# A fused FFT, MLP and routed-expert kernel: GpSimd's small operations one a step, and a shorter routing chain on VectorE

## The chip, the cores and the metric

One Trainium2 chip, one of its NeuronCores. The metric is the device time of one execution in microseconds (us). Three runs of the kernel before gave 3348.24, 3348.84 and 3351.0 us; the median is 3348.84 us. The engines are called PE (TensorE), DVE (VectorE), ACT (ScalarE), POOL (GpSimd) and SP (SyncE, which issues most transfers).

## What is computed

```python
X = np.fft.fft(x, axis=1); X = np.fft.fft(X, axis=2)     # x: 8 x 3072 x 256
x = X.real.reshape(24576, 256)
h = x @ w_in                                             # 256 -> 2048
g = h * np.clip(h + 3, 0, 6) / 6
x = g @ w_out                                            # 2048 -> 256
logits = x @ w_gate                                      # 8 experts
expert_idx = np.argmax(logits, axis=1)
probs = np.exp(logits - logits.max(-1, keepdims=True))
probs /= probs.sum(-1, keepdims=True) + 1e-09
# each token goes to its one expert: relu(x @ w1[e]) @ w2[e], times its probability
```

## The kernel before

The program has two parts. The first, to about 2150 us, does the Fourier transforms, the MLP and the routing; it ends with every token's row stored in a DRAM table `xs_dram` that is sorted by expert. The second reads tiles of that table and applies the experts. The change touches the first part alone.

**Batches, chunks, steps.** The first part runs over 8 batches, each of 6 chunks of 512 tokens, each of 8 steps: 384 steps in all. A step `s` (`step`, from L942) does for one pair of the 16 slices of the hidden width:

- PE: `mm1` writes the step's two halves into the PSUM tile `ab` (14 products with `WA`, `WB`, `XN`), and `mm2` of three steps before (LAG = 3) multiplies `gh` and `gl` with `WO` into `acc` (24 products, L513). `ab` has two buffers, which the transforms' products (`f`, `fe`, `fo`) and the routing's products share.
- ACT copies one half to `A` (L496); DVE makes `h` with a difference (L184) and a sum (L181) of `A` and `ab`; ACT makes `r` (L501), DVE multiplies it by `h` (L508), ACT rounds the product to `gh` (L959), and POOL writes what was rounded off to `gl` (L184, two operations a step). `r` has four buffers, two a step, so ACT's `r` of a step needs the buffer that `gl` of two steps before reads.

**Fill work.** Lists by step (`fill`, `pfill`, `afill`) hold everything else. For the next batch's transform `plan_folds` (L697) puts 40 operations of DVE on chosen steps: the folds of four input quarters `R` (774 or 516 columns), of their sums `H`, and splits into `SC0`, `SC1`, `SS0`, `SS1`. After a quarter's four folds POOL makes four sums `H<-R`, all in the step after the last fold. `R` has two buffers; SP loads a quarter when the sums of the quarter two before have been made.

**Routing** (`routing`, L542) follows each chunk: `s0` (maximum, difference, exponential), `s1` (one-hot `rt_oh` of the chosen expert), `s2` (POOL: running counts `rt_oc`, `cnt`), four steps later `s3_mm` (PE: rank of each token within its expert, two products) and `s3` (DVE: base + rank, times the one-hot, summed over experts to a row number `pi`; the sum of the exponentials and its reciprocal; the destination copied into the row), and four times `s4` (POOL: an indirect store of 128 rows of `xp` to `xs_dram`).

**Order.** A scheduler sets each engine's order from the program and its own estimate of readiness, except for what is pinned (`in_order`, `keep_in_program_order`: the folds stay in the written order among themselves). Each engine then works strictly in its order.

Of the kernel before, what the change touches and what calls it, by code (L numbers as in the profile page):

```python
# [10 lines left out]
F32 = mybir.dt.float32  # L11
# [35 lines left out]
BUFS = dict(h=2, r=4, gh=4, gl=4)  # L47
EXTRA = 23
LATE = (0, 0, 1, 1, 2, 3, 3, 4, 5, 5, 6, 6, 7, 7, 8, 8, 8, 9)
# [25 lines left out]
def tile_fft_moe(ctx, tc, xr, xf, xcoef, w_in, w_out, w_gate, w1, w2, tabs, fm, misc, tri, sgn8, dstc, maskc, out):  # L75
# [55 lines left out]
    w128 = pc.tile([P, KF], F32, name="w128")  # L131
    trib = pc.tile([P, P], BF16, name="trib")

# [4 lines left out]
    ssel = pc.tile([P, 1], F32, name="ssel")  # L138
    base8 = pc.tile([P, 4, NE], F32, name="base8")
    iom8 = pc.tile([P, 4, NE], F32, name="iom8")  # L140
# [39 lines left out]
    def add(eng, o, a, b):  # L180
        pinned(eng.tensor_tensor(out=o, in0=a, in1=b, op=ALU.add))  # L181

# [161 lines left out]
    def load_consts():  # L344
        sp.dma_start(ident, misc[:, 0:P])
        sp.dma_start(iot, misc[:, P:P + 2])
        sp.dma_start(itile, misc[:, P + 2:P + 2 + NTILE])
        o = P + 2 + NTILE
        sp.dma_start(cmask, misc[:, o:o + 64].rearrange("p (a c) -> p a c", a=NE))
        o += 64  # L350
        sp.dma_start(base8, misc[:, o:o + 32].rearrange("p (a c) -> p a c", a=4))
        o += 32
        sp.dma_start(iom8, misc[:, o:o + 32].rearrange("p (a c) -> p a c", a=4))
        o += 32
        sp.dma_start(dst_sb, dstc)
# [186 lines left out]
    def routing(xo, xp, t0, nt, mask, tagn, wait=RKW):  # L542
# [5 lines left out]
        def s0():  # L548
            st["m"] = m = sm("rt_m", [P, 4])
            st["d"] = d = sm("rt_d", [P, 4, NE])  # L550
            dve.tensor_reduce(out=m[:, 0:nt], in_=L, axis=AX.X, op=ALU.max)
            dve.tensor_tensor(out=d[:, 0:nt], in0=L, in1=bc(m), op=ALU.subtract)
            st["ex"] = ex = sm("rt_ex", [P, 4, NE])
            act.activation(ex[:, 0:nt], d[:, 0:nt], AF.Exp)

# [11 lines left out]

        def s2():
            st["oc"] = oc = sm("rt_oc", [P, 4, NE], BF16)
            oh = st["oh"]  # L570
            pool.tensor_copy(oc[:, 0], cnt)
            for t in range(nt):
                o = oc[:, t + 1] if t + 1 < nt else cnt
                pool.tensor_tensor(out=o, in0=oc[:, t], in1=oh[:, t], op=ALU.add)

        def s3_mm():
            ab = hold["ride"][:, 1] if hold.get("ride") is not None else bank(f"rk{tagn}")
            st["r"] = r = ab[:, 384:384 + nt * NE]
            mm_group(r, [(trib, st["oh"][:, 0:nt].rearrange("p t e -> p (t e)")),
                         (onesb, st["oc"][:, 0:nt].rearrange("p t e -> p (t e)"))])  # L580

        def s3():
            k = st["k"]
            r = st["r"].rearrange("p (t e) -> p t e", e=NE)
            dve.tensor_tensor(out=k[:, 0:nt], in0=base8[:, 0:nt], in1=r, op=ALU.add)
            s = sm("rt_s", [P, 4])
            dve.tensor_reduce(out=s[:, 0:nt], in_=st["ex"][:, 0:nt], axis=AX.X, op=ALU.add)
            dve.tensor_tensor(out=k[:, 0:nt], in0=k[:, 0:nt], in1=st["oh"][:, 0:nt], op=ALU.mult)
            dve.tensor_scalar(s[:, 0:nt], s[:, 0:nt], 1e-9, None, op0=ALU.add)
            ps = sm("rt_p", [P, 4])  # L590
# [13 lines left out]

        return [("f", s0), ("f", s1), ("f", s2)] + [("f", lambda: None)] * wait + [("p", s3_mm, s3)] + [("f", lambda t=t: s4(t)) for t in range(nt)]

    if True:
# [94 lines left out]
        def plan_folds(b):  # L702
# [225 lines left out]
        def step(s):  # L928
# [21 lines left out]
            if 0 < s <= NS:  # L950
                h = hold.pop(("h", s - 1))
                r, gh, gl = halves("r", F32, s), halves("gh", F32R, s), halves("gl", F32R, s)
                g = r
                for n in range(2):
                    relu6(r[n], h[n])
                for n in range(2):
                    gate_h(g[n], r[n], h[n])
                for n in range(2):
                    act.activation(gh[n], g[n], AF.Copy)  # L959
                for n in range(2):  # L960
                    sub(pool, gl[n], g[n], gh[n])
                hold[("g", s - 1)] = (gh, gl)
# [179 lines left out]
def _constants():  # L1142
# [26 lines left out]
    for c in range(1, 128):  # L1169
# [7 lines left out]
            np.tile((np.arange(8)[None, :] <= np.arange(8)[:, None]).astype(float).reshape(1, 64), (P, 1)),  # L1177
            np.tile((np.arange(8.0) * CAPR + TS)[None, None], (P, 4, 1)).reshape(P, 32),
# [3 lines left out]
    tri = (p[:, None] < p[None, :]).astype(float)  # L1182
    sgn8 = np.where(p[None, :, None] // 2 == np.arange(NB)[:, None, None], (-1.0) ** n, 0.0)
# [96 lines left out]
```

## Time and profile before

| | |
|---|---|
| median of three runs | 3348.84 us |
| the profiled execution, its own time | 3351.21 us |
| its span, first to last instruction | 3349.4 us |
| busy in the span | PE 94%, DVE 68%, POOL 68%, ACT 58% |
| 350 to 1903 us, batches 1 to 6 | 1553 us: PE 1439.95 busy, DVE 1189.59, POOL 1112.91, ACT 991.01 |
| the same stretch, ACT waiting for POOL's `gl` | 151.0 us in 53 waits |

How to read it: busy time overlaps between engines, and a busy PE is not one at its peak, since matmuls are pipelined. The waits are put down to what came last. In the stretch from 350 to 1903 us the same pattern of 48 steps comes six times. In a timeline row the first number is the start, the second the duration, and the bracket the idle time of the engine before it with what ended it.

### The profile page before, as it was taken

The numbers are of one execution on the slowest core, as the hardware profiler recorded it, in microseconds if no ns is written. First come the engines' busy times: TensorE is split into PE (matmuls) and PEld (weight loads), VectorE is DVE, ScalarE is ACT, GpSimd is POOL, SyncE is SP. The second block draws the span as 40 slices with busy tenths as digits, with TensorE's granted clock in tenths as the row PEclk, the third lists the DMA queues.
The fourth block names the chain that finished last, engine by engine and source line by source line (L and its number), as shares of the span: only waits on it lengthen the run. The fifth ranks groups of instructions, "written<-read, shape, count | busy, mean of one in ns | idle before, by whom it ended". The sixth has DMA issues, their size and how long they took to land.

```text
span 3349.4 us, 62616 instructions
## 1 busy us (share of the span) xinstructions
PE 3133.1 (94%) x23482; PEld 3001.7 (90%) x23482; DVE 2277.1 (68%) x3699; ACT 1934.1 (58%) x3339; POOL 2267.7 (68%) x1784
## 2 busy tenths in 40 slices
PE   5899999999999999999899999999999999999998
PEld 5899999899899899899899999988888888898887
DVE  8878777777777777777777676755555555555553
ACT  3566666566666566666566666645454444544453
POOL 5567776776776777677777776766676666666664
PEclk8999999999999999999999999999999999999999
DMA  5100100100100110000000002065555555545560
GB/s 180 61 28 21 36 25 14 43 24 16 39 28 16 33 33 16 30 30 17 31 14 16 14 18 51 20 193 154 144 168 149 143 149 158 147 145 154 147 171 30
DMA packets 256195, 243.18 MB, mean 73 GB/s; under 512 B 157739, under 2 KB 219020, under 8 KB 255888
## 3 DMA queue, kind: packets, MB, share of 16 engines
q1 hardware_dynamic: 234640, 184.66, 19.7%
q0 software_dynamic: 21248, 54.48, 4.5%
q8 instruction: 187, 3.06, 0.4%
q14 instruction: 120, 0.98, 0.1%
HBM read 159.71 MB, written 54.04 MB: 64 GB/s over the span
## 4 chain that ended last, share of the span: by engine, by line
PE 45%; DVE 18%; ACT 17%; issue 9%; POOL 5%; SPq 0%; DMA 0%; ACTq 0%; POOLq 0%; DVEq 0%
PE op L165 16%; PE hp L165 15%; PE acc L513 8%; ACT gh L959 7%; ACT r L501 6%; PE ab L165 5%; DVE h L184 4%; POOL gl L184 3%; DVE r L508 2%; POOL xs_dram L149 2%; DVE R L189 2%; DVE R L181 2%; DVE H L181 1%; ACT xp L539 1%; ACT xo L532 1%
## 5 line engine op out<-in xcount | busy, mean ns | idle before, releaser
L184 POOL TENSOR_TENSOR gl<-r,gh 128x512 fp32r<-128x512 f32 x768 | 1109.6, 1464 | 468.1 <-ACT gh L959 372.7
L501 ACT ACTIVATE r<-h,half 128x512 f32<-128x512 f32 x768 | 546.4, 719 | 610.1 <-DVE h L184 386.0
L508 DVE SCALAR_TENSOR_TENSOR r<-r,h 128x512 f32<-128x512 f32 x768 | 625.1, 818 | 369.3 <-ACT r L501 368.2
L513 PE MATMUL acc<-WO,gh 128*128 128x264 f32 x6144 | 824.4, 287 | 3.4 <-ACT xo L532 3.4
L513 PEld LDWEIGHTS acc<-WO,gh 128*128 128x128 f32 x6144 | 786.2, 192 | 3.6 <-ACT xo L532 3.6
L165 PE MATMUL ab<-pq,WA 128*128 128x256 f32 x2304 | 398.8, 290 | 107.4 <-DVE h L181 68.4
L995 DVE SCALAR_TENSOR_TENSOR WB<-hp,WA 128x512 fp32r<-128x512 f32 (+1 forms) x472 | 278.5, 606 | 301.8 <-ACT WA L994 301.7
L959 ACT ACTIVATE gh<-r 128x512 fp32r<-128x512 f32 x768 | 451.1, 622 | 42.6 <-DVE r L508 13.6
L513 PE MATMUL acc<-WO,gl 128*128 128x264 f32 x3072 | 444.6, 286 | 2.7 <-POOL gl L184 1.8
L165 PEld LDWEIGHTS ab<-pq,WA 128*128 128x128 f32 x2304 | 333.6, 193 | 120.3 <-issue 87.3
L513 PEld LDWEIGHTS acc<-WO,gl 128*128 128x128 f32 x3072 | 404.6, 189 | 6.1 <-POOL gl L184 5.6
L994 ACT ACTIVATE WA<-hp 128x512 fp32r<-128x512 f32 (+1 forms) x472 | 240.9, 529 | 197.5 <-PE hp L165 194.3
L165 PE MATMUL ab<-pq,WB 128*128 128x256 f32 x2304 | 349.2, 289 | 0.0
L149 POOL DMA_INDIRECT out_dram<-yo,dst x200 | 217.3, 1086 | 155.9 <-DVE yo L1095 118.3
L165 PEld LDWEIGHTS ab<-pq,WB 128*128 128x128 f32 x2304 | 314.2, 197 | 0.0
L149 POOL DMA_INDIRECT xs_dram<-xp,pic x192 | 212.6, 1107 | 125.6 <-DVE pic L599 68.9
L165 PE MATMUL hp<-xTb,TB 128*128 128x512 f32 (+1 forms) x1344 | 277.8, 364 | 13.9 <-DVE WB L995 13.9
L165 PE MATMUL hp<-xTa,W1b 128*128 128x512 f32 (+1 forms) x1392 | 277.0, 358 | 2.2 <-DVE WB L995 2.2
L165 PEld LDWEIGHTS hp<-xTb,TB 128*128 128x128 f32 x1344 | 226.3, 188 | 58.1 <-DVE WB L995 15.5
L165 PE MATMUL op<-W2b,WA 128*128 128x256 f32 x1536 | 276.3, 282 | 0.0
L165 PEld LDWEIGHTS hp<-xTa,W1b 128*128 128x128 f32 x1392 | 228.8, 189 | 43.3 <-DVE WB L995 2.6
L184 DVE TENSOR_TENSOR h<-A,ab 128x512 f32<-128x512 f32 x384 | 259.4, 675 | 6.7 <-ACT A L496 6.1
(269 smaller groups left out, 5479.7 us busy)
## 6 DMA issues: line engine op xcount, KB each, us to landing
w1a<-in_w_dram SPq DMA_DIRECT2D x29, 1024.0 KB
w1b<-in_w_dram SPq DMA_DIRECT2D x29, 1024.0 KB
w2b<-in_w_dram SPq DMA_DIRECT2D x58, 512.0 KB
R<-in_xr_dram SPq DMA_DIRECT2D x32, 774.0 KB
w2a<-in_w_dram SPq DMA_DIRECT2D x29, 768.0 KB
w2d<-in_w_dram SPq DMA_DIRECT2D x28, 256.0 KB
q<-pq SPq DMA_DIRECT2D x288, 1.0 KB
raw<-in_w_in_dram SPq DMA_DIRECT2D x8, 512.0 KB
```

Of the source, the lines that this page charges most:

```text
L149: i = pool.indirect_dma_start(oob_is_err=False, **kw)
L165: pe.matmul(dst, l, r, start=(n == 0), stop=(n == len(terms) - 1))
L181: pinned(eng.tensor_tensor(out=o, in0=a, in1=b, op=ALU.add))
L184: i = eng.tensor_tensor(out=o, in0=a, in1=b, op=ALU.subtract)
L189: pinned(dve.scalar_tensor_tensor(out=o, in0=a, scalar=s, in1=b, op0=ALU.mult, op1=ALU.add))
L501: act.activation(r, h, AF.Relu, bias=half, scale=1.0 / 6.0)
L508: dve.scalar_tensor_tensor(out=g, in0=r, scalar=1.0, in1=h, op0=ALU.min, op1=ALU.mult)
L513: pe.matmul(acc[t][:, 0:GW], lhs, wo(w, f0 + i), start=st, stop=sp_)
L532: act.activation(xo[:, t, :], acc[t][:, 0:GW], AF.Copy)
L959: act.activation(gh[n], g[n], AF.Copy)
L994: act.activation(hi, ps, AF.Relu)
L995: dve.scalar_tensor_tensor(out=lo, in0=ps, scalar=0.0, in1=hi, op0=ALU.max, op1=ALU.subtract)
```

## The change

POOL's small operations are tied to the step they are written in, and the routing's arithmetic is rearranged.

- `behind(i)` adds an ordering, without a wait, that puts an operation of POOL behind the newest `gl`. The indirect stores, the counts and the sums `H<-R` are all put behind it.
- `s2` becomes five entries of one step each (copy and first count together), in place of one entry and four empty steps; `s3` and `s4` keep their steps. The four sums of a quarter stand in four steps in place of one.
- The experts' base rows, split into two exactly held parts, are appended to the constant `trib`; a third product adds them to the ranks on PE, and the addition of `base8` on DVE falls away.
- 1e-9 stands as a ninth column beside the eight exponentials, so the separate addition falls away.
- The destination is copied by ACT in `s0`, no longer by DVE in `s3`.
- The sum over experts writes the integer row number itself, and the cast falls away (in the chunks with a mask, the last scalar operation writes it).
- `EXTRA`, the step in the last batch at which a left-over row is handled, goes from 23 to 25.

```diff
+    def behind(i):
+        tc.add_manual_dep(i.ins, hold["gl"].ins.name, mybir.DependencyInfo(mybir.DependencyClass.NoSync, mybir.DependencyReason.DATA),
+                          reason="one a step")
+
     def scat(group, **kw):
         i = pool.indirect_dma_start(oob_is_err=False, **kw)
+        if group == "xs":
+            behind(i)
...
-            st["ex"] = ex = sm("rt_ex", [P, 4, NE])
-            act.activation(ex[:, 0:nt], d[:, 0:nt], AF.Exp)
+            act.activation(ex9s[nt][:, :, 0:NE], d[:, 0:nt], AF.Exp)
+            act.activation(xp.bitcast(F32)[:, 0:nt, D + 1:XW], dst_sb[:, t0:t0 + nt, None].to_broadcast([P, nt, XW - D - 1]), AF.Copy)
...
-        def s2():
-            st["oc"] = oc = sm("rt_oc", [P, 4, NE], BF16)
-            oh = st["oh"]
-            pool.tensor_copy(oc[:, 0], cnt)
-            for t in range(nt):
-                o = oc[:, t + 1] if t + 1 < nt else cnt
-                pool.tensor_tensor(out=o, in0=oc[:, t], in1=oh[:, t], op=ALU.add)
+        def s2(t):
+            if t == 0:
+                st["oc"] = sm("rt_oc", [P, 4, NE], BF16)
+                behind(pool.tensor_copy(st["oc"][:, 0], cnt))
+            oc = st["oc"]
+            o = oc[:, t + 1] if t + 1 < nt else cnt
+            behind(pool.tensor_tensor(out=o, in0=oc[:, t], in1=st["oh"][:, t], op=ALU.add))
...
+                         (onesb, trib[:, P:P + nt * NE])])
...
-            dve.tensor_tensor(out=k[:, 0:nt], in0=base8[:, 0:nt], in1=r, op=ALU.add)
+            dve.tensor_tensor(out=k[:, 0:nt], in0=r, in1=st["oh"][:, 0:nt], op=ALU.mult)
+            st["pi"] = pi = pw.tile([P, 4], I32, tag=f"rt_pi{nt}", name=f"pi{tagn}")
+            ps = pi if mask is None else sm("rt_p", [P, 4])
+                dve.tensor_reduce(out=ps[:, 0:nt], in_=k[:, 0:nt], axis=AX.X, op=ALU.add)
             s = sm("rt_s", [P, 4])
-            dve.tensor_reduce(out=s[:, 0:nt], in_=st["ex"][:, 0:nt], axis=AX.X, op=ALU.add)
-            dve.tensor_tensor(out=k[:, 0:nt], in0=k[:, 0:nt], in1=st["oh"][:, 0:nt], op=ALU.mult)
-            dve.tensor_scalar(s[:, 0:nt], s[:, 0:nt], 1e-9, None, op0=ALU.add)
-            ps = sm("rt_p", [P, 4])
-            dve.tensor_reduce(out=ps[:, 0:nt], in_=k[:, 0:nt], axis=AX.X, op=ALU.add)
+            dve.tensor_reduce(out=s[:, 0:nt], in_=ex9s[nt], axis=AX.X, op=ALU.add)
             dve.reciprocal(xp.bitcast(F32)[:, 0:nt, D], s[:, 0:nt])
...
-            dve.tensor_copy(xp.bitcast(F32)[:, 0:nt, D + 1:XW], dst_sb[:, t0:t0 + nt, None].to_broadcast([P, nt, XW - D - 1]))
-            dve.tensor_copy(pi[:, 0:nt], ps[:, 0:nt])
...
-        return [("f", s0), ("f", s1), ("f", s2)] + [("f", lambda: None)] * wait + [("p", s3_mm, s3)] + [("f", lambda t=t: s4(t)) for t in range(nt)]
+        return [("f", s0), ("f", s1)] + [("f", lambda t=t: s2(t) if t < nt else None) for t in range(wait + 1)] + [("p", s3_mm, s3)] + [("f", lambda t=t: s4(t)) for t in range(nt)]
...
-                for f in o[9 * hf + 5:9 * hf + 9]:
-                    fill[u0 + at[n + 3] + 1].append(lambda f=f: in_order(f))
+                for k, f in enumerate(o[9 * hf + 5:9 * hf + 9]):
+                    fill[u0 + at[n + 3] + 1 + k].append(lambda f=f: behind(f()))
```

POOL's order, stores and counts of one chunk (`rt_oc` and `cnt` are the counts, `pic` the row numbers). Before:

```order
L571 COPY rt_occ_11364<-cnt 128x8
L184 TENSOR_TENSOR gl_0_11212<-r_0_11208,gh_0_11210 128x512
L184 TENSOR_TENSOR gl_1_11213<-r_1_11209,gh_1_11211 128x512
L149 DMA xs_dram<-xp_10565,pic_11156 198656x260 x4
L184 TENSOR_TENSOR gl_0_11281<-r_0_11277,gh_0_11279 128x512
L184 TENSOR_TENSOR gl_1_11282<-r_1_11278,gh_1_11280 128x512
L574 TENSOR_TENSOR rt_occ_11364<-rt_occ_11364,rt_ohc_11299 128x8 x3
L574 TENSOR_TENSOR cnt<-rt_occ_11364,rt_ohc_11299 128x8
```

and now:

```order
L155 DMA xs_dram<-xp_7681,pic_8262 198656x260
L194 TENSOR_TENSOR gl_0_8389<-r_0_8385,gh_0_8387 128x512
L194 TENSOR_TENSOR gl_1_8390<-r_1_8386,gh_1_8388 128x512
L155 DMA xs_dram<-xp_7681,pic_8262 198656x260
L194 TENSOR_TENSOR gl_0_8459<-r_0_8455,gh_0_8457 128x512
L194 TENSOR_TENSOR gl_1_8460<-r_1_8456,gh_1_8458 128x512
L155 DMA xs_dram<-xp_7681,pic_8262 198656x260
L582 COPY rt_occ_8473<-cnt 128x8
L585 TENSOR_TENSOR rt_occ_8473<-rt_occ_8473,rt_ohc_8407 128x8
L194 TENSOR_TENSOR gl_0_8531<-r_0_8527,gh_0_8529 128x512
L194 TENSOR_TENSOR gl_1_8532<-r_1_8528,gh_1_8530 128x512
L155 DMA xs_dram<-xp_7681,pic_8262 198656x260
```

A `gl` pair no longer stands behind four stores or four counts, but behind one store and at most two counts.

POOL's order, the four sums of a quarter `R_0_0`, which free its buffer for the load of `R_1_0`. Before:

```order
L181 TENSOR_TENSOR H_0_9996<-R_0_0_9994 128x2x129
L184 TENSOR_TENSOR H_0_9996<-R_0_0_9994 128x2x129
L184 TENSOR_TENSOR H_0_9996<-R_0_0_9994 128x129
L181 TENSOR_TENSOR H_0_9996<-R_0_0_9994 128x129
L184 TENSOR_TENSOR gl_0_10859<-r_0_10855,gh_0_10857 128x512
```

and now, from the second sum to the fourth:

```order
L194 TENSOR_TENSOR H_0_9946<-R_0_0_9944 128x2x129
L155 DMA xs_dram<-xp_9937,pic_10522 198656x260
L585 TENSOR_TENSOR rt_occ_10736<-rt_occ_10736,rt_ohc_10670 128x8
L194 TENSOR_TENSOR gl_0_10859<-r_0_10855,gh_0_10857 128x512
L194 TENSOR_TENSOR gl_1_10860<-r_1_10856,gh_1_10858 128x512
L194 TENSOR_TENSOR H_0_9946<-R_0_0_9944 128x129
L585 TENSOR_TENSOR rt_occ_10736<-rt_occ_10736,rt_ohc_10670 128x8
L194 TENSOR_TENSOR gl_0_10921<-r_0_10917,gh_0_10919 128x512
L194 TENSOR_TENSOR gl_1_10922<-r_1_10918,gh_1_10920 128x512
L189 TENSOR_TENSOR H_0_9946<-R_0_0_9944 128x129
```

The last sum now stands three steps after the first, two steps of DVE ahead of the first fold of `R_1_0`.

DVE's order, `s3` of one chunk (`f` is the PSUM tile that holds the ranks). Before:

```order
L598 COPY xp_11134<-dst_sb 128x4x3
L322 TENSOR_TENSOR pf_1_0_11142<-f_1_0_11097,vc_1_0_11141 128x256
L323 TENSOR_TENSOR pf_1_0_11142<-f_1_0_11097,vc_1_0_11141 128x256
L585 TENSOR_TENSOR rt_kc_10725<-base_103,f_1_0_11097 128x32
L184 TENSOR_TENSOR h_0_11202<-A_11204,ab_11159 128x512
L588 TENSOR_TENSOR rt_kc_10725<-rt_kc_10725,rt_ohc_10729 128x32
L181 TENSOR_TENSOR h_1_11203<-A_11204,ab_11159 128x512
L178 SCALAR_TENSOR_TENSOR pq_1_11096<-pf_1_0_11142,pq_1_11096 128x512
L591 TENSOR_REDUCE rt_pc_11153<-rt_kc_10725 128x4
L508 SCALAR_TENSOR_TENSOR r_0_11277<-r_0_11277,h_0_11202 128x512
L599 CAST pic_11156<-rt_pc_11153 128x4
```

and now:

```order
L332 TENSOR_TENSOR pf_1_0_11081<-f_1_0_11035,vc_1_0_11080 128x256
L333 TENSOR_TENSOR pf_1_0_11081<-f_1_0_11035,vc_1_0_11080 128x256
L597 TENSOR_TENSOR rt_kc_10666<-f_1_0_11035,rt_ohc_10670 128x32
L194 TENSOR_TENSOR h_0_11137<-A_11139,ab_11094 128x512
L601 TENSOR_REDUCE pic_11089<-rt_kc_10666 128x4
L189 TENSOR_TENSOR h_1_11138<-A_11139,ab_11094 128x512
L186 SCALAR_TENSOR_TENSOR pq_1_11034<-pf_1_0_11081,pq_1_11034 128x512
```

Row numbers are ready before the second `h`, one step's worth of DVE earlier, and three operations of this piece are gone (the fourth, the addition of 1e-9, stood a few rows further on).

## Rows read from the trace of the kernel before

**Rows 1.** Windows, batches 1 to 6: busy of PE, PEld, DVE, ACT, POOL; clock; DMA share; GB/s.

```profile
350.00:1903.00 1553.00, 1439.95 (x11563) 1416.49 (x11562) 1189.59 (x1971) 991.01 (x1827) 1112.91 (x1003) 0.98 0.08 25
```

**Rows 2.** Groups by line on PE, 350 to 1903 us: busy us, mean ns.

```profile
L513 PE MATMUL acc<-WO,gh 128*128 128x264 f32 x4608 | 614.4, 286 | 0.0
...
L165 PE MATMUL f<-rt_occ,onesb 128*128 128x32 bf16 x24 | 4.2, 176 | 0.0
```

**Rows 3.** Timeline of PE, two starts of `mm1` in steps without a stall.

```profile
824.26 0.52 PE L165 MATMUL ab<-pq,WA 128*128 128x256 f32 x3
...
828.82 0.52 PE L165 MATMUL ab<-pq,WA 128*128 128x256 f32 x3
```

**Rows 4.** Waits, 350 to 1903 us: total us, times, longest.

```profile
ACT r L501 <- POOL gl L184: 151.0, 53, 4.0
...
PE ab L165 <- DVE h L181: 60.1, 43, 2.3
```

**Rows 5.** Timeline of DVE, one step without a fold and one with.

```profile
821.94 0.67 DVE L184 TENSOR_TENSOR h<-A,ab 128x512 f32<-128x512 f32 x1
...
825.80 0.67 DVE L184 TENSOR_TENSOR h<-A,ab 128x512 f32<-128x512 f32 x1
...
828.98 0.76 DVE L508 SCALAR_TENSOR_TENSOR r<-r,h 128x512 f32<-128x512 f32 x1 [0.96 <-ACT r L501]
...
831.63 0.67 DVE L184 TENSOR_TENSOR h<-A,ab 128x512 f32<-128x512 f32 x1
```

**Rows 6.** Timeline of POOL: a `gl` pair on time; then the first of four stores, and the next `gl` pair.

```profile
833.72 2.99 POOL L184 TENSOR_TENSOR gl<-r,gh 128x512 fp32r<-128x512 f32 x2 [2.83 <-ACT gh L959]
...
899.96 1.19 POOL L149 DMA_INDIRECT xs_dram<-xp,pic  x1 [1.60 <-DVE pic L599]
...
905.43 2.56 POOL L184 TENSOR_TENSOR gl<-r,gh 128x512 fp32r<-128x512 f32 x2
```

**Rows 7.** Timeline of ACT, the two `r` after that burst.

```profile
906.78 0.72 ACT L501 ACTIVATE r<-h,half 128x512 f32<-128x512 f32 x1 [3.39 <-POOL gl L184]
...
911.68 0.72 ACT L501 ACTIVATE r<-h,half 128x512 f32<-128x512 f32 x1 [2.04 <-POOL gl L184]
```

**Rows 8.** Timeline of DVE: a fold beside `gl`, then the same piece.

```profile
870.63 1.77 DVE L181 TENSOR_TENSOR R<-R 128x516 f32<-128x516 f32 x1
...
902.00 0.18 DVE L559 SCALAR_TENSOR_TENSOR rt_kc<-rt_dc,iom 128x32 f32<-128x32 f32 x1
902.10 0.17 DVE L587 TENSOR_REDUCE rt_sc<-rt_exc 128x4 f32<-128x32 f32 x1
...
903.81 0.69 DVE L189 SCALAR_TENSOR_TENSOR R<-R 128x516 f32<-128x516 f32 x1
904.41 0.68 DVE L184 TENSOR_TENSOR h<-A,ab 128x512 f32<-128x512 f32 x1
...
907.54 1.01 DVE L508 SCALAR_TENSOR_TENSOR r<-r,h 128x512 f32<-128x512 f32 x1 [1.85 <-ACT r L501]
...
910.42 0.67 DVE L184 TENSOR_TENSOR h<-A,ab 128x512 f32<-128x512 f32 x1
```

**Rows 9.** Groups by line and form on DVE, 350 to 1903 us: busy us, mean ns.

```profile
L508 DVE SCALAR_TENSOR_TENSOR r<-r,h 128x512 f32<-128x512 f32 x576 | 452.7, 789 | 292.3 <-ACT r L501 291.8
...
L181 DVE TENSOR_TENSOR R<-R 128x516 f32<-128x516 f32 x23 | 28.8, 1253 | 0.0
L588 DVE TENSOR_TENSOR rt_kc<-rt_kc,rt_ohc 128x32 f32<-128x32 f32 x36 | 19.8, 550 | 0.0
```

**Rows 10.** Timeline and windows, a load of `R`: POOL's last sum, windows after it, DVE's first fold.

```profile
868.04 0.41 POOL L181 TENSOR_TENSOR H<-R 128x129 f32<-128x129 f32 x1
...
870.00:872.00 2.00, 2.00 (x18) 1.88 (x16) 2.00 (x2) 0.15 (x1) 1.85 (x2) 1.00 0.89 342
872.00:874.00 2.00, 1.15 (x9) 0.97 (x9) 1.75 (x4) 0.90 (x2) 0.00 (x0) 1.00 0.08 21
...
881.74 2.04 DVE L181 TENSOR_TENSOR R<-R 128x774 f32<-128x774 f32 x1
```

More of the change, by code (lines that the diff above doesn't have):

```diff
@@ L47 @@
 BUFS = dict(h=2, r=4, gh=4, gl=4)
-EXTRA = 23
+EXTRA = 25
 LATE = (0, 0, 1, 1, 2, 3, 3, 4, 5, 5, 6, 6, 7, 7, 8, 8, 8, 9)
@@ L131, in tile_fft_moe @@
     w128 = pc.tile([P, KF], F32, name="w128")
-    trib = pc.tile([P, P], BF16, name="trib")
+    trib = pc.tile([P, P + 4 * NE], BF16, name="trib")
+    ex9s = {n: pc.tile([P, n, NE + 1], F32, name=f"ex{n}") for n in (4, 1)}
     XN = pc.tile([P, 8 * P], F32R, name="XN")
@@ L138, in tile_fft_moe @@
     ssel = pc.tile([P, 1], F32, name="ssel")
-    base8 = pc.tile([P, 4, NE], F32, name="base8")
     iom8 = pc.tile([P, 4, NE], F32, name="iom8")
@@ L180, in add @@
     def add(eng, o, a, b):
-        pinned(eng.tensor_tensor(out=o, in0=a, in1=b, op=ALU.add))
+        i = eng.tensor_tensor(out=o, in0=a, in1=b, op=ALU.add)
+        pinned(i)
+        return i
     def sub(eng, o, a, b):
@@ L350, in load_consts @@
         o += 64
-        sp.dma_start(base8, misc[:, o:o + 32].rearrange("p (a c) -> p a c", a=4))
-        o += 32
         sp.dma_start(iom8, misc[:, o:o + 32].rearrange("p (a c) -> p a c", a=4))
@@ L364, in start_tables @@
         dve.memset(cnt, 0.0)
+        for t in ex9s.values():
+            dve.memset(t, 1e-9)
     def load_tables():
@@ L578, in s3_mm @@
             st["r"] = r = ab[:, 384:384 + nt * NE]
-            mm_group(r, [(trib, st["oh"][:, 0:nt].rearrange("p t e -> p (t e)")),
-                         (onesb, st["oc"][:, 0:nt].rearrange("p t e -> p (t e)"))])
+            mm_group(r, [(trib[:, 0:P], st["oh"][:, 0:nt].rearrange("p t e -> p (t e)")),
+                         (onesb, st["oc"][:, 0:nt].rearrange("p t e -> p (t e)")),
+                         (onesb, trib[:, P:P + nt * NE])])
         def s3():
@@ L584, in s3 @@
             r = st["r"].rearrange("p (t e) -> p t e", e=NE)
-            dve.tensor_tensor(out=k[:, 0:nt], in0=base8[:, 0:nt], in1=r, op=ALU.add)
-            s = sm("rt_s", [P, 4])
-            dve.tensor_reduce(out=s[:, 0:nt], in_=st["ex"][:, 0:nt], axis=AX.X, op=ALU.add)
-            dve.tensor_tensor(out=k[:, 0:nt], in0=k[:, 0:nt], in1=st["oh"][:, 0:nt], op=ALU.mult)
-            dve.tensor_scalar(s[:, 0:nt], s[:, 0:nt], 1e-9, None, op0=ALU.add)
-            ps = sm("rt_p", [P, 4])
-            dve.tensor_reduce(out=ps[:, 0:nt], in_=k[:, 0:nt], axis=AX.X, op=ALU.add)
+            dve.tensor_tensor(out=k[:, 0:nt], in0=r, in1=st["oh"][:, 0:nt], op=ALU.mult)
+            st["pi"] = pi = pw.tile([P, 4], I32, tag=f"rt_pi{nt}", name=f"pi{tagn}")
+            ps = pi if mask is None else sm("rt_p", [P, 4])
+            with nc.allow_low_precision(reason="one term of the sum is not zero, and all are whole"):
+                dve.tensor_reduce(out=ps[:, 0:nt], in_=k[:, 0:nt], axis=AX.X, op=ALU.add)
+            s = sm("rt_s", [P, 4])
+            dve.tensor_reduce(out=s[:, 0:nt], in_=ex9s[nt], axis=AX.X, op=ALU.add)
             dve.reciprocal(xp.bitcast(F32)[:, 0:nt, D], s[:, 0:nt])
@@ L595, in s3 @@
                                          op0=ALU.mult, op1=ALU.add)
-                dve.tensor_scalar(ps[:, 0:nt], ps[:, 0:nt], BIG, None, op0=ALU.add)
-            st["pi"] = pi = pw.tile([P, 4], I32, tag=f"rt_pi{nt}", name=f"pi{tagn}")
-            dve.tensor_copy(xp.bitcast(F32)[:, 0:nt, D + 1:XW], dst_sb[:, t0:t0 + nt, None].to_broadcast([P, nt, XW - D - 1]))
-            dve.tensor_copy(pi[:, 0:nt], ps[:, 0:nt])
+                dve.tensor_scalar(pi[:, 0:nt], ps[:, 0:nt], BIG, None, op0=ALU.add)
         def s4(t):
@@ L710, in plan_folds @@
                 at[n] = max(at[n], FFT_AT[2][1] + 1 + (n - 24) // 2)
+            assert at[7] + 4 <= at[12] and at[21] + 4 <= at[28]
             assert at[32] < FFT_AT[0][0] and at[39] < FFT_AT[1][0] + 6 * STEPS
@@ L960, in step @@
                 for n in range(2):
-                    sub(pool, gl[n], g[n], gh[n])
+                    hold["gl"] = sub(pool, gl[n], g[n], gh[n])
                 hold[("g", s - 1)] = (gh, gl)
@@ L1177, in _constants @@
             np.tile((np.arange(8)[None, :] <= np.arange(8)[:, None]).astype(float).reshape(1, 64), (P, 1)),
-            np.tile((np.arange(8.0) * CAPR + TS)[None, None], (P, 4, 1)).reshape(P, 32),
             np.tile((np.arange(8.0) - 8)[None, None], (P, 4, 1)).reshape(P, 32),
@@ L1181, in _constants @@
     misc = np.concatenate(cols, 1)
-    tri = (p[:, None] < p[None, :]).astype(float)
+    base = np.tile(np.arange(8.0) * CAPR + TS, 4)
+    parts = np.zeros((P, 32))
+    parts[0] = base // 8192 * 8192
+    parts[1] = base % 8192
+    assert (parts % 256 == 0).all()
+    tri = np.concatenate([(p[:, None] < p[None, :]).astype(float), parts], 1)
     sgn8 = np.where(p[None, :, None] // 2 == np.arange(NB)[:, None, None], (-1.0) ** n, 0.0)
```

## Prediction

> **What bounds the kernel now.** I read four views in this order: the page, the windows and groups of the stretch in which the batches repeat, the waits of that stretch, and the timelines of one chunk. The page puts PE at 94% and DVE and POOL at 68%, so a first glance says PE. The windows and groups correct that. Six batches take 1553 us [rows 1] and hold 4608/16 = 288 steps [rows 2], so a step takes 5.39 us, while PE alone, unstalled, needs 4.56 us from one `mm1` to the next [rows 3]. That is 38 products, 0.12 us each. The transforms add 95 products a batch (four pieces of 14, one of 13, one of 26), 95 x 0.12 x 6 = 68 us. PE's floor is 288 x 4.56 + 68 = 1381 us; the stretch is **172 us** above it.
>
> What holds PE up is named by the waits: `ab`, waiting for DVE's `h` [rows 4]. The timelines say why DVE is late. In a step without a fold DVE goes from `h` to `h` in 825.80 - 821.94 = 3.86 us, in one with a fold in 831.63 - 825.80 = 5.83 us [rows 5]. Idle time stands inside both (0.96 us for the second `r`), so it is a loop of DVE and ACT that a fold lengthens by its whole duration. Steps without a fold are shorter than PE's, those with one longer, and with two buffers of `ab` the two don't average out. In the list of ACT's waits in this stretch PE does not appear as a releaser of `A`. So **the loop of DVE and ACT is the bound from 350 to 1903 us**, and what it gains counts until PE's floor is reached. The second part of the program is not touched.
>
> **How POOL comes into the loop.** A `gl` pair on time takes 2.99 us [rows 6], and then POOL waits. After the routing it is not on time: the first of four stores starts at 899.96 us (after 1.60 us of waiting for the row numbers), and the next pair only at 905.43 us [rows 6]. ACT's next `r` needs the buffer which that pair reads; it starts at 906.78 us after 3.39 us of idling, and a later one at 911.68 us after 2.04 us [rows 7]. There are 53 such waits, 151 us [rows 4]. Not all of it is loss: without POOL the two `r` would have waited for `h`, ready at 904.41 + 0.68 = 905.09 us and 910.42 + 0.67 = 911.09 us [rows 8]. The excess is 1.7 + 0.6 = 2.3 us of 5.4.
>
> **The change, part by part.** All sums are over the 36 chunks of batches 1 to 6. Batch 0 has other fill work and the last batch has no folds; I put both at nothing, which errs to the small side.
>
> *Stores, counts and sums one a step.* With the stores between the pairs, a pair stands behind one store. The excess goes: 151 x 2.3/5.4 = **-64 us**. Its bounds are 0 (all of it covered by other lateness) and -151. A late pair also lies beside DVE's `r`, which then takes 1.01 us [rows 8] and not 0.76 [rows 5]. The mean over 576 is 0.789 [rows 9], some 0.07 above the mean of 0.69 and 0.76, so 40 us in all; half of them lie behind bursts, **-20 us**, bounds 0 and -40.
>
> *What POOL on time gives back.* A fold costs more when it meets `gl`: 516 columns took 0.69 us at 903.81, while POOL stored, and 1.77 us at 870.63, beside a `gl` pair [rows 8]: 1.08 more. The mean of that group is 1.253 [rows 9], so (1.253 - 0.69)/1.08 = 52% of them are met today. Bursts are one cause of free folds, since stores don't hold a fold up. In the piece shown, the fold behind the first late `r` would now meet `gl`. I count one newly met fold per chunk: 36 x 1.08 = **+39 us**. Bounds: 0, and 75 us if all free ones meet (24 long folds a batch, 144 in six, 48% of them are 69, x 1.08).
> The Trainium skill (SBUF — State Buffer, Who interferes with whom) says that a VectorE instruction with two SBUF inputs and a GpSimd one that reads SBUF exclude each other, and the later one waits for the whole of the other. By that rule it speaks against this change: a POOL that is always on time meets every fold that stands between two `r`, and the sum would carry +75 instead of +39. That is the second rival below.
>
> *Routing on DVE.* Small operations follow each other at 0.10 us [rows 8]; four fewer are 0.4 us a chunk. The product L588 has a mean of 0.55 us [rows 9] because it meets `gl`; the one in its place reads PSUM, and I take 0.18 us for it, as for its neighbour [rows 8]: 0.37. Together 0.77 x 36 = **-28 us**, bounds -40 (the copy also waits for ACT now) and 0 (where the operation after it waits for ACT in any case). The row number is ready before the second `h`, so the first store has nothing to wait for.
>
> *What is added.* The third product costs at most its 0.176 us [rows 2], under 9 us over the kernel, on an engine with 172 us to spare: 0 now, up to +9 if PE becomes the bound. ACT's copy of 12 columns stands behind the exponential, after `A`; ACT waits for DVE there soon after, which covers it. If that cover went, 49 x 0.2 = 10 us. The counts are spread, but only routing's product four steps later reads them: 0.
>
> *A load that now starts late.* The sums free the buffer for the third quarter's load. Today the last one ends at 868.45 us, the data come between 870 and some 872.2, and the fold starts at 881.74: 9 us in hand [rows 10]. Now the last sum stands three steps later, behind the `gl` pair two steps of DVE before that fold. A pair on time ends at 833.72 + 2.99 = 836.71, 7.0 us after its own `r` (828.98 + 0.76) [rows 5, 6]; with the sum and 4 us of load that makes 11.4 after `r`, while DVE would be at the fold after one step with a fold and half of one without, some 7.7 us [rows 5]. DVE stands for 3 to 4 us once a batch. It regains the 0.96 that it would wait for `r`, and the fold then runs free. Net 2 us, six times: **+12 us**, bounds 0 and +24.
> SP's queue holds little behind that load: the loads of `q` that follow are for later chunks.
>
> Sum: -64 - 20 + 39 - 28 + 12 = **-61 us**. The profiled execution took 3351.21 us, its span 3349.4 us; 3351.2 - 61 = 3290. It stands 2.4 us above the median of the runs, 3348.84, so the runs should come at 3288 us. -61 is a third of PE's 172, so PE does not cap it.
>
> **Rivals.**
> *A. The folds stay free* (no give-back, since DVE is behind ACT after the routing and keeps its place): -61 - 39 = -100, 3249 us; with the bounds on the excess it could go on to PE's floor, 172 below, 3177. For it: PE's floor is far. Against: in steps on time every fold shown is met.
> *B. All long folds meet* `gl`: -61 + 75 - 39 = -25, 3324 us; if a quarter of the excess was covered by other lateness besides, +16 more, 3340. For it: half are met even now. Against: a DVE that is behind ACT after the routing comes to its folds when the pair is done. By the skill's rule named above this is the case to expect.
> *C. Slower: POOL becomes the bound in the four steps with a store.* A pair of 2.99, a store of 1.19 and its 0.30 of issue, a sum of 0.41 make 4.9 us [rows 6, 10], more than the 3.86 us of a loop step without a fold [rows 5]. `gl` would be late in four steps a chunk rather than 1.5: 4 x 1.0 x 36 = 144 us, in place of the -84 that vanish: -28 + 39 + 12 + 144 - 84 = +83, 3432 us at most. It decides where four steps in a row are shorter than 4.9 us. Against it: the steps behind the routing hold folds and average 5.4, and the buffers of `r` leave about one microsecond.
> *D. POOL's lateness is only a sign*, DVE being late there by its own work; gain and give-back cancel, 3340 to 3355 us. That the order would not change is ruled out by the rows of order.
>
> **How the numbers follow.** Forecast (3270 to 3320) 0.50, A below 3270 0.20, B with part of the excess covered (3320 to 3342) 0.17, D 0.06, C 0.07. The range takes the forecast, B, and A to a little below its own time: 3245 to 3338 us. Under 0.2%, 6.7 us, a measurement of this kernel can't tell from no change: faster 0.87, same 0.06, slower 0.07.
>
> **What would show it.** Right: ACT's waits for POOL's `gl` fall from 151 us to under 50 in the six batches; a batch takes about 249 us instead of 259; stores stand singly between `gl` pairs; the mean of `R` folds of 516 columns rises from 1.25 towards 1.5; DVE waits 3 to 4 us for the load of `R` once a batch. The excess is mis-sized if the waits vanish but the batch shrinks by under 5 us. Wrong: waits for POOL that stay, or a PE that waits for nothing (then A).

## The result, and the profile after

The changed kernel takes **3383.19 us** (median of 4 runs, 3381.32 to 3385.33), the kernel before 3348.54 beside it: a ratio of 1.0103, 95% interval 1.0085 to 1.012. It is slower by 34.6 us where 61 us less was forecast, and lies outside the range. The profiled execution took 3384.44 us, its span 3382.7.

The loss is where the gain was expected. Batches 1 to 6 lie between 353 and 1930 us and take 24 us more than before [rows 1]; of the rest, some 3 us are in batch 0 and 7 in the last batch, and the second part takes no longer than before. First the window, then the waits (total us, times, longest) of this stretch:

```profile
353.00:1930.00 1577.00, 1442.25 (x11597) 1421.79 (x11596) 1242.81 (x1827) 992.34 (x1863) 1117.13 (x1007) 0.98 0.08 25
```

```profile
DVE r L518 <- ACT r L511: 235.4, 409, 1.6
PE ab L173 <- DVE h L189: 96.8, 57, 5.2
...
DVE R L189 <- DMA R<-in_xr_dram: 22.6, 6, 4.0
...
DVE pf L332 <- ACT vc L331: 10.7, 18, 1.1
ACT r L511 <- POOL gl L194: 9.5, 6, 1.6
```

The change did what it says: ACT's waits for `gl` fell from 151.0 us to 9.5 [rows 4]. Yet DVE is busy for 1242.81 us and not 1189.59 [rows 1], 53 us more, with 144 instructions fewer. Its idle time fell by 29 us only. 53 - 29 = 24: the whole loss of the stretch. The groups of DVE, by line and form (busy us, mean ns, idle time before them), say in which operations it lies. After:

```profile
L518 DVE SCALAR_TENSOR_TENSOR r<-r,h 128x512 f32<-128x512 f32 x577 | 496.3, 866 | 235.4 <-ACT r L511 235.4
...
L569 DVE SCALAR_TENSOR_TENSOR rt_kc<-rt_dc,iom 128x32 f32<-128x32 f32 x36 | 31.2, 867 | 0.0
...
L189 DVE TENSOR_TENSOR R<-R 128x774 f32<-128x774 f32 x22 | 26.5, 1205 | 22.6 <-DMA R<-in_xr_dram 22.6
L573 DVE SCALAR_TENSOR_TENSOR rt_ohc<-rt_ixc,iom 128x32 bf16<-128x32 f32 x36 | 25.2, 699 | 0.0
...
L189 DVE TENSOR_TENSOR R<-R 128x516 f32<-128x516 f32 x23 | 22.3, 969 | 0.0
...
L186 DVE SCALAR_TENSOR_TENSOR SS1s<-H,SS1s 128x258 fp32r<-128x258 f32 x12 | 13.1, 1094 | 0.0
```

And the three of them that were not shown of the kernel before:

```profile
L563 DVE SCALAR_TENSOR_TENSOR rt_ohc<-rt_ixc,iom 128x32 bf16<-128x32 f32 x36 | 6.9, 190 | 0.0
...
L559 DVE SCALAR_TENSOR_TENSOR rt_kc<-rt_dc,iom 128x32 f32<-128x32 f32 x36 | 6.4, 178 | 0.0
...
L178 DVE SCALAR_TENSOR_TENSOR SS1s<-H,SS1s 128x258 fp32r<-128x258 f32 x12 | 5.0, 418 | 0.0
```

The same `r`, 452.7 us before [rows 9], now takes 43.6 us more. Two small operations of the routing, 0.18 and 0.19 us each before, take 0.87 and 0.70 us: 43 us more. None of these was changed. All of them have two inputs in SBUF. The other groups together give 34 of these 87 us back, above all the operations that the routing no longer has; 53 remain. A timeline shows one of the slow `r`, POOL first, then DVE:

```profile
1015.15 1.29 POOL L155 DMA_INDIRECT xs_dram<-xp,pic  x1
1016.47 0.21 POOL L585 TENSOR_TENSOR rt_occ<-rt_occ,rt_ohc 128x8 bf16<-128x8 bf16 x1
1016.63 2.52 POOL L194 TENSOR_TENSOR gl<-r,gh 128x512 fp32r<-128x512 f32 x2
```

```profile
1014.53 1.02 DVE L518 SCALAR_TENSOR_TENSOR r<-r,h 128x512 f32<-128x512 f32 x1 [0.91 <-ACT r L511]
1016.19 3.52 DVE L518 SCALAR_TENSOR_TENSOR r<-r,h 128x512 f32<-128x512 f32 x1 [0.64 <-ACT r L511]
1019.63 0.68 DVE L194 TENSOR_TENSOR h<-A,ab 128x512 f32<-128x512 f32 x1
```

With the store and the count ahead of it the pair begins at 1016.63 us, just behind the start of the second `r`. That `r` ends at 1019.71 us, after both halves of the pair, at 1019.15; it takes 3.52 us where one on time takes 0.76 [rows 5].

### The profile page after: what moved, and what is told of

It reads as the page before. It is cut to its first block, busy times and chain, and to the rows that moved or that the text cites. A ratio compares the mean times of both kernels' runs of the same rounds, so it can differ in the third digit from the quotient of the medians.

```text
span 3382.7 us, 62560 instructions
## 1 busy us (share of the span) xinstructions
PE 3136.3 (93%) x23531; PEld 3007.5 (89%) x23531; DVE 2334.6 (69%) x3505; ACT 1935.1 (57%) x3388; POOL 2267.9 (67%) x1784
## 5 line engine op out<-in xcount | busy, mean ns | idle before, releaser
L194 POOL TENSOR_TENSOR gl<-r,gh 128x512 fp32r<-128x512 f32 x768 | 1084.3, 1430 | 596.1 <-ACT gh L969 491.9
L518 DVE SCALAR_TENSOR_TENSOR r<-r,h 128x512 f32<-128x512 f32 x768 | 680.2, 892 | 300.8 <-ACT r L511 299.8
L173 PE MATMUL hp<-xTb,TB 128*128 128x512 f32 (+1 forms) x1344 | 277.2, 364 | 13.6 <-DVE WB L1005 13.6
L194 DVE TENSOR_TENSOR h<-A,ab 128x512 f32<-128x512 f32 x384 | 259.4, 676 | 11.5 <-ACT A L506 11.2
L189 DVE TENSOR_TENSOR h<-A,ab 128x512 f32<-128x512 f32 x384 | 259.6, 676 | 0.0
```

What stands on the lines that cost most here:

```text
L173: pe.matmul(dst, l, r, start=(n == 0), stop=(n == len(terms) - 1))
L189: i = eng.tensor_tensor(out=o, in0=a, in1=b, op=ALU.add)
L194: i = eng.tensor_tensor(out=o, in0=a, in1=b, op=ALU.subtract)
L518: dve.scalar_tensor_tensor(out=g, in0=r, scalar=1.0, in1=h, op0=ALU.min, op1=ALU.mult)
```

## The experiments

The first theory, P, said: the new places on POOL cost all of it, and the smaller routing on DVE is a gain. Its rival Q: the smaller routing itself costs. "The stretch" below is batches 1 to 6, from their first `mm1` to the next batch's.

**1. routing_only.** The changed kernel with `behind` and the spreading taken back:

```diff
-EXTRA = 25
+EXTRA = 23
...
-        if group == "xs":
-            behind(i)
...
-                for k, f in enumerate(o[9 * hf + 5:9 * hf + 9]):
-                    fill[u0 + at[n + 3] + 1 + k].append(lambda f=f: behind(f()))
+                for f in o[9 * hf + 5:9 * hf + 9]:
+                    fill[u0 + at[n + 3] + 1].append(lambda f=f: in_order(f))
```

(and `s2` as one entry again, with its four additions).

> The kernel before with the smaller routing alone (exponentials into a tile with a preset 1e-9, destination copy on ACT, third product for the base, fewer VectorE operations); stores, counts, sums and the extra rows stand where they stood before. Theory P (the places on POOL cost all of the loss, the smaller routing is a gain): under 3349 by 15 to 38 us, so 3310 to 3334, and batches 1 to 6 near 256 us. Rival Q (the smaller routing itself costs, by ACT's copy and the operations that now read a PSUM tile): 3349 to 3375.

Measured: 3399.26 us, ratio 1.0151 (1.0138 to 1.0164). The time lies above both ranges. P, as it was stated, is out; but Q need not follow, for the timeline shows an order on POOL that the edit does not write. POOL, then DVE:

```profile
914.70 1.01 POOL L155 DMA_INDIRECT xs_dram<-xp,pic  x1 [2.56 <-DVE pic L599]
915.73 2.56 POOL L192 TENSOR_TENSOR gl<-r,gh 128x512 fp32r<-128x512 f32 x2
918.45 1.37 POOL L155 DMA_INDIRECT xs_dram<-xp,pic  x1 [0.17 <-issue]
...
922.56 2.54 POOL L192 TENSOR_TENSOR gl<-r,gh 128x512 fp32r<-128x512 f32 x2
```

```profile
915.54 2.81 DVE L567 SCALAR_TENSOR_TENSOR rt_kc<-rt_dc,iom 128x32 f32<-128x32 f32 x1
918.27 1.28 DVE L516 SCALAR_TENSOR_TENSOR r<-r,h 128x512 f32<-128x512 f32 x2
...
921.79 3.91 DVE L516 SCALAR_TENSOR_TENSOR r<-r,h 128x512 f32<-128x512 f32 x2
```

The scheduler now puts the first of the four stores ahead of a pair, and the pair between the first and the second store; the likely reason, not tested by itself, is that the smaller routing has its row numbers earlier. There the pair meets `rt_kc`, which takes 2.81 us instead of 0.18; the next pair meets two `r`, 3.91 us instead of 1.28.

**2. behind_only.** The kernel before with all the rest of the change (`behind`, spread counts and sums, `EXTRA` 25):

```diff
-EXTRA = 23
+EXTRA = 25
...
+        if group == "xs":
+            behind(i)
...
+                for k, f in enumerate(o[9 * hf + 5:9 * hf + 9]):
+                    fill[u0 + at[n + 3] + 1 + k].append(lambda f=f: behind(f()))
```

> The other half: stores, counts and sums one a step behind the low parts and the extra rows two steps later, with the old routing on VectorE. Theory P: slower than the changed kernel by what the routing gains, 3395 to 3420 us. Rival Q: between the two kernels, 3349 to 3375. If the two halves add up, the differences of this run and of the routing alone from the kernel before sum to +34.6 us.

Measured: 3400.25 us, ratio 1.0153 (1.014 to 1.0167). The two halves, 50 and 51 us each against the kernel before beside them, don't add up to 34.6. That each brings pairs to a bad place, and that together they don't do it twice, is my reading; no run shows it.

**3. stores_only.** Of the change, only the two lines in `scat` on the kernel before (and `behind` itself).

> The kernel before with the stores alone behind the low parts; counts and sums stay in one step each. Theory P: ACT's waits for POOL's gl fall as in the changed kernel, but VectorE's r and the small operations of the routing wait for the longer runs of POOL, so 3340 to 3370 us. Rival S (the stores carry the gain that the prediction put at 64 to 84 us, and the loss is in the sums and counts alone): 3270 to 3310.

Measured: 3388.51 us, ratio 1.0119 (1.0105 to 1.0134); slower than P's range, and rival S is out. DVE's and ACT's orders are those of before, and POOL's differs by the stores' places and, in some chunks, by a count's; so 39 us come from the place of the four stores on POOL.

**4. sums_together.** In the changed kernel the sums alone go back (the last four lines of the first diff).

> The changed kernel with the four sums of a quarter back in one step, in program order, as before; so the load of the third quarter is early again. Theory P1 (VectorE's stand of 3.7 us a batch for that load is loss in full, over six batches): 3383 - 22 = 3361 us, or lower if the spread sums also lengthened r. Rival P2 (most of the stand is regained, as the prediction had it, 2 us net a batch): 3371 us, and rival P3 (nothing of it counts): 3380 to 3386.

Measured: 3369.57 us, ratio 1.0062 (1.0049 to 1.0075): 13.6 us under the changed kernel. The load costs 22.6 us of waiting in the stretch (above); 13.6 of it, or 60%, is loss. P2, at 3371, is nearest. In this run's trace that wait is gone; the 13.6 are net of what else moved (`r` takes 505.6 us, and one fold a batch has another place in DVE's order).

**5. burst, and 6. burst_pair_later.** The new theory, P': four stores in a row do not hold DVE up (a fold beside them took 0.69 us [rows 8]), and in the kernel before they fall where DVE, behind the routing, catches up without waiting for ACT; they shelter it. In burst the scheduler is made to keep them together, behind the pair that they stood behind before; in the second run they come one entry later. Against routing_only:

```diff
+        if group == "xs":
+            behind(i)
...
-[("f", lambda t=t: s4(t)) for t in range(nt)]
+[("f", lambda: [s4(t) for t in range(nt)])]
```

> The kernel of the run routing_only (smaller routing on VectorE; counts, sums and extra rows as before) with one difference on POOL: the four stores of a chunk stand together behind the pair of low parts that they stood behind before, where routing_only has one store ahead of that pair. VectorE's and ACT's orders are those of routing_only. Theory P' (a burst of stores, which reads nothing beside VectorE, shelters VectorE while it catches up behind the routing; a pair in its place costs VectorE some 2.5 us a chunk): the 50 us of routing_only go and the gain of the smaller routing shows, 3310 to 3340 us. Rival Q (the smaller routing itself costs): within 10 us of routing_only, 3390 to 3410.

> As the run burst, with one more pair of low parts ahead of the four stores, so that a pair falls into the steps in which VectorE catches up and the burst comes after them. Theory P': that pair costs VectorE 1.5 to 2.8 us a chunk in 36 chunks, 54 to 100 us over the run burst, so 3375 to 3430. Rival L (what counts is how long the next low parts are late, which is the same four stores here): as the run burst, within 10 us of it.

Measured: burst 3343.64 us, ratio 0.9985 (0.9976 to 0.9994), **55.6 us under routing_only** with the same orders on DVE and ACT; POOL's differs by the place of the stores alone. burst_pair_later 3382.74, ratio 1.0102 (1.0086 to 1.0117), 39.1 above burst. So it is the place of a pair among DVE's catching up, not the routing, that costs. Rivals Q and L are out. Both effects were put too high: burst lies 4 us above its range, and the later pair costs 39 us where 54 to 100 were put. In burst_pair_later the pair meets two `r`, 2.52 us instead of 1.28, and a fold, 1.77 instead of 0.69 (POOL, then DVE):

```profile
915.39 2.97 POOL L194 TENSOR_TENSOR gl<-r,gh 128x512 fp32r<-128x512 f32 x2
```

```profile
914.70 2.52 DVE L518 SCALAR_TENSOR_TENSOR r<-r,h 128x512 f32<-128x512 f32 x2
917.14 1.77 DVE L199 SCALAR_TENSOR_TENSOR R<-R 128x516 f32<-128x516 f32 x1
```

The piece of routing_only again, in burst, POOL and DVE:

```profile
894.74 1.28 POOL L155 DMA_INDIRECT xs_dram<-xp,pic  x1 [0.16 <-issue]
896.32 0.98 POOL L155 DMA_INDIRECT xs_dram<-xp,pic  x1 [0.30 <-issue]
897.61 0.98 POOL L155 DMA_INDIRECT xs_dram<-xp,pic  x1 [0.30 <-issue]
898.89 1.30 POOL L155 DMA_INDIRECT xs_dram<-xp,pic  x1 [0.30 <-DVE xp L604]
900.18 0.55 POOL L585 TENSOR_TENSOR rt_occ<-rt_occ,rt_ohc 128x8 bf16<-128x8 bf16 x1
900.70 2.54 POOL L194 TENSOR_TENSOR gl<-r,gh 128x512 fp32r<-128x512 f32 x2
```

```profile
895.05 0.18 DVE L569 SCALAR_TENSOR_TENSOR rt_kc<-rt_dc,iom 128x32 f32<-128x32 f32 x1
895.15 1.28 DVE L518 SCALAR_TENSOR_TENSOR r<-r,h 128x512 f32<-128x512 f32 x2
896.36 0.69 DVE L189 TENSOR_TENSOR R<-R 128x516 f32<-128x516 f32 x1
...
898.68 1.39 DVE L518 SCALAR_TENSOR_TENSOR r<-r,h 128x512 f32<-128x512 f32 x2
899.99 0.69 DVE L199 SCALAR_TENSOR_TENSOR R<-R 128x516 f32<-128x516 f32 x1
```

For 5.4 us, 894.74 to 900.19, four `r`, two folds and the routing run at or within 0.15 us of their shortest. The pair behind them is late for it: ACT waits 116.1 us for `gl` in burst's stretch.

**7. glz_before, and 8. glz_routing.** How much do the low parts on POOL cost DVE in all? A memset in place of the subtraction, in the kernel before and in routing_only:

```diff
-                    sub(pool, gl[n], g[n], gh[n])
+                    pool.memset(gl[n].bitcast(F32), 0.0)
```

> The kernel before with the low parts set to zero by POOL's memset, which reads nothing; the third group of products is computed on zeros, so the low parts are left out of the result. Orders of VectorE and ACT are unchanged. It takes away both ACT's waits for POOL and the standing of VectorE beside a pair (37.9 us a batch over the shortest durations). Theory P' expects the batches to fall from 259 us to near PE's floor of 230, 3180 to 3260 us for the whole; if the standing costs VectorE nothing on its path, 3300 or more.

> The run routing_only with the same memsets in place of the low parts. Theory P': without pairs beside VectorE the smaller routing is a gain again, 0 to 38 us under the run glz_before (0 where PE is the bound). Rival Q: 30 to 60 us above it, as the two kernels stand to each other with their low parts.

Measured: 3150.2 us, ratio 0.9403 (0.9388 to 0.9418), and 3152.54, ratio 0.9413 (0.9396 to 0.9429). The low parts cost 198 us, ACT's waits for them and DVE's standing together; more could not show, since PE is the bound without them. Both times lie under what P' gave, 3180 to 3260, but the batches fall to PE's floor as it said. The window of glz_before:

```profile
340.00:1720.00 1380.00, 1380.00 (x11509) 1375.81 (x11509) 988.47 (x1964) 1011.46 (x1820) 550.34 (x997) 1.00 0.09 28
```

PE is busy without a gap in both runs, so it is the bound, and the second run says nothing of the routing. A batch takes 231 us in glz_before: that is the prediction's floor of PE, 1381/6 = 230.

**9. stores_new** is burst with the stores one a step, each behind a pair (`s4` as in the first diff's kernel). **10. between** puts each of them between the two halves of the next step's pair, to test theory W, that DVE waits out POOL's whole run of operations; **11. stores_late** has the later step alone.

```diff
+                hold["gl"] = sub(pool, gl[0], g[0], gh[0])
+                first_ = hold.pop("mid", [])
+                for f in first_:
+                    f()
+                hold["gl"] = sub(pool, gl[1], g[1], gh[1])
...
+[("f", lambda t=t: hold.setdefault("mid", []).append(lambda: s4(t)) if t0 < 4 * NCH - 8 else s4(t)) for t in range(nt)]
```

> The kernel of the run burst with the four stores one a step, each behind a pair of low parts, instead of together; counts, sums and extra rows as before. Theory P' (a pair among VectorE's catching up costs, whatever the routing): as the stores alone on the old routing, 30 to 45 us over the run burst, 3374 to 3389. Rival: with the smaller routing VectorE is less behind and the spread stores fit, within 10 us of burst.

> The run stores_new with each store put between the two halves of a pair of low parts (the pair of the next step) instead of behind a pair. Theory W (a VectorE operation with two SBUF inputs waits until POOL's run of operations that follow each other without a gap ends, and not for one of them): it now gets in behind the first half, no r, row or one-hot operation in these steps waits over 1.4 us, and the time lies 15 to 60 us under stores_new. Rival (it waits for one operation whatever follows): within 10 us of stores_new.

> The run stores_new with each store one step later, behind the pair of that step; VectorE's order is that of stores_new. It differs from the run between by the place of one half of a pair alone. If the gain of between comes from the halves being apart: within 10 us of stores_new, 3366 to 3386. If it comes from the later step: within 10 us of between, 3338 to 3358.

Measured: stores_new 3376.36, ratio 1.0074 (1.006 to 1.0088), 33 us over burst, as P' has it, and by the stores' places alone; between 3348.09, ratio 0.9993 (0.9984 to 1.0002); stores_late 3381.53, ratio 1.0095 (1.0081 to 1.011). The place of one half of a pair is worth 33 us, 27 of them in batches 1 to 6, where the orders of DVE and ACT are the same in both. The rival to W, one operation whatever follows, is out. But W's limit of 1.4 us does not hold: `r` of between still takes up to 3.80 us, beside three halves in a row (rows in the last section). One piece of stores_late and the same of between (POOL, DVE) shows what the store between does:

```profile
1053.97 2.99 POOL L194 TENSOR_TENSOR gl<-r,gh 128x512 fp32r<-128x512 f32 x2 [1.49 <-ACT gh L969]
...
1055.73 1.78 DVE L189 TENSOR_TENSOR H<-H 128x516 f32<-128x516 f32 x1
```

```profile
1041.25 1.29 POOL L199 TENSOR_TENSOR gl<-r,gh 128x512 fp32r<-128x512 f32 x1 [2.31 <-ACT gh L974]
1042.70 1.27 POOL L159 DMA_INDIRECT xs_dram<-xp,pic  x1 [0.16 <-PE ab L178]
...
1043.01 0.69 DVE L194 TENSOR_TENSOR H<-H 128x516 f32<-128x516 f32 x1
```

The fold comes while POOL stores, and takes 0.69 us instead of 1.78. In other steps the second half and an `r` meet instead: over the stretch `r` takes 550.5 us in between and 523.5 in stores_late, while DVE's idle time before it is 201.4 us in between and 242.5 in stores_late. How the 33 us divide between these is not settled.

**12. burst_counts** (changed kernel, stores and sums together, counts spread), **13. between_counts** (sums_together with the stores between the halves) and **14. sums_only** (of the change only the spread sums, on the kernel before).

> The changed kernel with the four stores of a chunk together again and the four sums together; the counts stay spread, one a step, and the extra rows two steps later. If theory P' is whole (only the pairs among the catching up and the load of R cost): as the run burst, 3335 to 3350 us. If the spread counts help or cost by themselves, they show as the distance from burst.

> The changed kernel with the four sums together and each store between the halves of the next step's pair; the counts stay spread. It stands to the run sums_together as between stands to stores_new. If halves apart are a gain of their own: 20 to 40 us under sums_together, 3330 to 3350. If the gain of between hung on the place of the counts or on the later step meeting other work there: within 10 us of sums_together.

> The kernel before with the four sums of a quarter spread over four steps, each behind a pair, and nothing else. Theory P1 (VectorE's stand for the late load is loss in full): 6 x 3.8 = 23 us, 3371. The prediction's term: 2 net a batch, 12, so 3361. Hidden: 3349. Below 3349: the four sums in a row make low parts late in some steps today, and spreading them gains more than the load costs.

Measured: burst_counts 3361.36, ratio 1.0031 (1.0019 to 1.0043), 18 us over burst; between_counts 3358.57, ratio 1.0025 (1.0015 to 1.0035), 11 us under sums_together, between its two expectations; sums_only 3366.92, ratio 1.005 (1.0036 to 1.0063), 16 us over the kernel before beside it, between the prediction's 12 and the 23 of its whole wait.

So P' as stated is not the whole: burst_counts lies 11 us above the range that it was given. The 18 us lie in batches 1 to 6, where the orders of DVE and ACT are those of burst and POOL's differs by the counts alone (the extra rows belong to the last batch). In burst a count of 0.55 us stands between the four stores and the next pair, which starts at 900.70 us, just as the fold of 899.99 ends (above). With the counts elsewhere the pair follows the last store at once, and meets that fold, which takes 3.32 us instead of 0.69 (burst_counts, POOL, then DVE):

```profile
908.26 2.55 POOL L194 TENSOR_TENSOR gl<-r,gh 128x512 fp32r<-128x512 f32 x2
```

```profile
908.05 3.32 DVE L199 SCALAR_TENSOR_TENSOR R<-R 128x516 f32<-128x516 f32 x1
```

Over the stretch these folds take 45.3 us instead of 28.9, and the one-hot of L573 28.5 instead of 13.0. So whether a burst shelters DVE hangs on where the next pair falls, here on half a microsecond. With spread counts, four stores together (burst_counts) and one a step (sums_together, the same orders on DVE and ACT) both take 1564 us in batches 1 to 6; with the counts together it is 1547 us (burst) and 1573 (stores_new).

## Why the prediction was wrong

*The bound, right.* The loop of DVE and ACT sets the stretch, and PE's floor is where it was put (glz_before).

*Excess of POOL's lateness, -64: near in size.* The waits for `gl` went, and DVE's idle time before `r` fell from 291.8 to 235.4 us, by 56 [rows 9]. How much of the 56 is the excess is not shown: an operation that stands longer also leaves less to wait for.

*"A late pair also lies beside DVE's `r`", -20: the step that failed.* It came out as **+43.6**. I read `r`'s standing as a mark of POOL's bursts, so that it would go with them. In truth a pair behind one store and a count is late by some 1 us (in the piece shown it begins at 1016.63, when ACT had been done with `gh` at 1015.55), which is where the second `r` stands, and the pair behind four stores in the kernel before comes after DVE has caught up. The burst that I counted as a cost was a shelter there (stores_only, 39 us).

*Folds newly met, +39: it did not come.* The four groups of `R` took 122.7 us before and 112.2 after; with the two of `H` of 516 columns all long folds took 188.5 and 184.3. The pairs met `r` and the small operations instead. The sentence on the Trainium skill's rule (SBUF — State Buffer, Who interferes with whom) put this exclusion at +75 and on the folds alone; the trace agrees that it decides, with 0.18 us turned into 2.81. The hold was longer than that sentence has it, for the small operation waited for both instructions of the pair. And it fell on `r` and the routing's smallest operations, not on the folds alone.

*Routing, -28.* The removed operations did go, but L569 and L573 now stand in the pairs' way and give back 43 us. `pf` waits 10.7 us for ACT, where DVE's own copy, which is gone, had waited 10.0 before, so that wait stayed and the copy's own time was all there was to gain. That the first store then "has nothing to wait for" was booked as harmless; with the smaller routing by itself a store stood ahead of a pair, and that place cost some 50 us (routing_only, and burst, which puts it back). In burst, where the places are kept, routing is worth 4.6 us over the whole kernel.

*Load of `R`, +12: right in kind.* The wait was 3.8 us a batch as forecast; 13.6 to 16 us net come from it (sums_together, sums_only).

*The rivals.* B has the mechanism nearest to this, pairs that meet DVE, but on the folds and with a gain left over. C expected to be slower by ACT's waits for `gl`, which are gone. A and D, no give-back and no change, are out by the time. None let the smaller operations meet the pair.

*The signs.* The waits under 50 us, the single stores and the 3 to 4 us for the load came; a batch of 249 us (it takes 263) and a mean rising towards 1.5 us for the `R` folds of 516 columns (0.97 and 1.06) did not.

Counted over the stretch: idle -29 us (`r` -56, load +23, the rest ACT), busy +53.

## What to carry to other kernels

Where two engines exclude each other, an engine that is late in bursts may be sheltering the other; before spreading its work, look at what the other engine runs in the burst, and price every operation, also those of 0.2 us, that will now stand beside it. When a scheduler orders the work, an edit on one engine can move an instruction past another on a third: compare that engine's order, and pin the old one, before judging the edit. Here half a microsecond in the place of a pair was enough. The best version here is burst: the smaller routing with the stores kept together, 0.15% under the kernel before.

## What the runs showed of the hardware

Not expected: a DVE operation with two SBUF inputs did not get in between the two halves of a pair where they followed each other without a gap. In the changed kernel the `r` of 1016.19 us waited for both (3.52 us); in routing_only a `rt_kc` that elsewhere takes 0.18 us and that began at 915.54, 0.19 us before the pair, ended after it. In the run between, two `r` that start 0.65 us before a single half of 1.30 us, while a store still runs, take 3.11 us and not 1.28, 1.83 more (POOL, then DVE):

```profile
944.81 1.00 POOL L159 DMA_INDIRECT xs_dram<-xp,pic  x1 [0.16 <-issue]
945.85 1.30 POOL L199 TENSOR_TENSOR gl<-r,gh 128x512 fp32r<-128x512 f32 x1
947.10 2.15 POOL L590 TENSOR_TENSOR rt_occ<-rt_occ,rt_ohc 128x8 bf16<-128x8 bf16 x3
```

```profile
945.20 3.11 DVE L523 SCALAR_TENSOR_TENSOR r<-r,h 128x512 f32<-128x512 f32 x2
```

Counts that follow a half without a gap are not waited out: here three of them, 2.15 us together, start at 947.10, and the two `r` end before them, at 948.31. In the same run two `r` beside three halves in a row take 4.39 us and end behind the third; the longer of them is the 3.80 us of above (POOL, then DVE):

```profile
1005.34 3.79 POOL L199 TENSOR_TENSOR gl<-r,gh 128x512 fp32r<-128x512 f32 x3
```

```profile
1005.89 4.39 DVE L523 SCALAR_TENSOR_TENSOR r<-r,h 128x512 f32<-128x512 f32 x2 [0.25 <-ACT r L516]
```

Whether the wait begins in the tail of the store ahead, as these rows suggest, was not tried. The store itself held nothing up: in burst a fold at 896.36 us, beside one, took 0.69 us.
